# A new order of TensorE's units and new list priorities in a fused attention and MLP kernel

## The chip, the cores and the metric

The kernel runs on one core of a Trainium2 chip. The metric is device time in microseconds (us), from the start of one execution to its end. Three runs of the kernel before took 804.34, 805.24 and 806.07 us.

## The reference, cut to what matters

```python
# x: 2048 tokens x 512; 32 heads of 128; 8 memory rows; segments of 32 tokens
def _A_ref(x, mem0, Wq, Wk, Wv, Wo, seg_len):
    mask = (idx[:, None] < M) | (idx[:, None] >= idx[None, :])
    mem = mem0
    for s in range(n_seg):                       # 64 segments, one after the other
        xs = x[:, s * seg_len:(s + 1) * seg_len, :]
        h = jnp.concatenate([mem, xs], axis=1)   # 8 + 32 rows
        q, k, v = (einsum('btd,dhe->bhte', h, W) for W in (Wq, Wk, Wv))
        p = _softmax(where(mask, einsum('bhqe,bhke->bhqk', q, k) * scale, -1e9))
        o = einsum('bhte,hed->btd', einsum('bhqk,bhke->bhqe', p, v), Wo)
        mem = o[:, :M, :]                        # goes into the next segment
        outs.append(o[:, M:, :])
h  = x + _A_ref(_layernorm(x), ...)
y  = _layernorm(_layernorm(h))
h2 = h + gelu(y @ w1 + b1) @ w2 + b2             # 512 -> 1792 -> 512
```

Weights, inputs and output are bf16. The eight memory rows make the 64 segments a chain: no segment's queries, keys and values are complete before the output projection of the one before it.

## The kernel before, in words

**Segments.** The kernel treats the last 24 tokens of each memory-plus-segment window apart from the rest. For segment s, the tile `hT` holds, transposed, 24 token rows and the 8 memory rows. The other 8 rows of the segment (`hB`) don't depend on memory and are projected for four segments at once, one group of four ("bank") ahead; this work is called F.

TensorE's work in a segment is cut into *units*, with these names. Q0, Q1, K0, K1, V0, V1 (`passes`, line 796): a projection of half of the heads, four units each; a unit is four matmuls of 512 columns side by side in four column tiles of 32 (written 128\*32 in the profile). F0 and F1: in three segments of a bank, the Q, K or V projection of `hB`, four units each, of the same form; in the fourth segment `wo_B` (line 1112), eight units in F1's name. In the last bank F0 and F1 are the MLP's first matmuls instead (`w1_first`, line 1233), plain 128\*128 matmuls. In the first bank F is four dummy matmul units (`warm`, line 765). SC0 and SC1 (`sc_mm`, line 963): scores of the memory queries, for half of the heads each; behind each stands a softmax (`sc_softmax`: maximum `nmc` L972 on VectorE, exponentials `EC` L976 on ScalarE, reciprocal `rsc` L979, product `PC` L982 and a transpose into `PTC` L983 on VectorE). PV0 and PV1 (`pv_c`, lines 994 and 998): probabilities times values for these; they and PVA run in row tiles of 32 (32\*128). SA (`sa_mm`, line 1025): scores of the 24 token rows, one unit; its softmax ends in `PTA`. PVA (`pv_a`, line 1055), two units: probabilities times values of the segment before. WO (`wo`, line 1083): the output projection, eight units; VectorE transposes its result (`TT`, L1095) and adds its halves into the memory rows of the next `hT` (L1089).

Projections go from PSUM to `kq` (a copy on ScalarE or VectorE, lines 814 and 815) and through a VectorE transpose (L839) into `KALL` and `QT`; queries are copied into `ZC`. V goes to `VS`.

**Order.** TensorE's order is written out: `ORDERS` gives for each *place* a list of `unit.from.to`. A place is a1 to a3 for segments 1 to 3, m0 to m3 for segments 4 to 59 by s modulo 4 (14 segments each), and z60 to z63 for the last four. Segment 0 (`START`) and the MLP behind segment 63 have orders of their own. `TURNED` says in which places a projection goes through its four units backwards; where two neighbouring units use the same weights, the second doesn't load them.

The order of the other engines comes from a list scheduler (`Sched.schedule`) that runs when the kernel is built. It takes operations by rank, that is by the longest modelled way from an operation to the end, plus a *bonus* from the table `BONUS` by the kind of its output and its place ("PTC1@m0"). It places each at the earliest free time of its engine, by modelled durations (`dur`), by a modelled signal time (`HOP`) and a cost for a turn between tile forms (`SWITCH`). Some copies may go to ScalarE or VectorE, whichever ends earlier. On the chip each engine runs its list in order and waits on semaphores.

```python
heapq.heappush(heap, (-o.rank - BONUS.get(o.key, BONUS.get(o.kind, 0.0)), pos[o], o.gidx, o))   # Sched.schedule
...
for n, lo, hi in [(u, int(x), int(y)) for u, x, y in (w.split(".") for w in ORDERS.get(place(s), "").split())]:
    S.take((s, n), lo, hi)          # TensorE's own list
```

`align` counts TensorE's instructions (`ni` of each unit: 8 for a projection unit, 4 if weights are kept, 32 for SC and for a half of PVA, 40 for PV, 16 for WO, 64 for SA). It counts in blocks of 256 (`FETCH_N`), and pads the first units of each m0 segment with repeated weight loads until the third unit's place in its block is `LOCK` = 106.

Of the kernel before, what the change touches and what calls it, by code (L numbers as in the profile page):

```python
# [1599 lines left out]
```

## Time and profile before

| what | value |
|---|---|
| median of three runs (lowest, highest) | 805.24 us (804.34, 806.07) |
| span of the profiled execution | 802.2 us |
| median less span | 3.0 us |
| TensorE busy | 775.9 us, 97% of the span |
| VectorE busy | 600.7 us, 75% |
| ScalarE busy | 558.0 us, 70% |
| GpSimd busy | 90.1 us, 11% |
| mean granted TensorE clock | 0.998 |
| LDWEIGHTS instructions | 20880, 423.1 us |

The span runs from the first to the last instruction of the profiled execution; that execution's time as a run isn't given on its own, so its span is set against the median of the runs. A matmul's end in the profile is modelled, and neighbours overlap: for pace, one reads the starts. In the timeline a row with "x8" merges eight matmuls, two units of four. Lines 547 and 796 are both projection units, with and without a weight load. The segments begin at about 48 us and end at about 700 us; the MLP follows.

### The profile page before, as it was taken

To read this page: it belongs to the slowest core of one execution; us is meant where nothing else is said; L and a number is where in the kernel's file an instruction comes from. 1 tells how busy PE (TensorE), PEld (TensorE's weight loads), DVE (VectorE), ACT (ScalarE), POOL (GpSimd) and SP (SyncE) were. 2 spreads that over 40 slices of the span, in tenths; PEclk is the share of its full clock that TensorE was granted. 3 is DMA by queue.
4 is the path that set the end of the run, shared out by engine and by line. 5 is a ranking of instruction groups with operands and counts; after the bars stand their busy time and mean duration, and the time that the engine had idled before them with its cause. 6 is when DMAs were issued, how large, how long until landed. Compare 5 with 4: busy or idle time off the path is not lost.

```text
span 802.2 us, 46835 instructions
## 1 busy us (share of the span) xinstructions
PE 775.9 (97%) x21699; PEld 423.1 (53%) x20880; DVE 600.7 (75%) x1847; ACT 558.0 (70%) x1580; POOL 90.1 (11%) x211
## 2 busy tenths in 40 slices
PE   2899999999999999999999999999999999999998
PEld 1455555555555555555555555555555555644444
DVE  3277878888888888888888888888888888732311
ACT  1557777777777777777778777777777777773342
POOL 5022000010001010101010101000000000020700
PEclk9999999999999999999999999999999999999999
DMA  9961010201111121102010202010212112074300
GB/s 367 394 174 24 4 37 11 45 12 37 26 33 30 30 33 27 36 19 42 19 43 15 49 12 50 13 37 20 50 25 56 51 38 59 17 232 127 86 27 26
DMA packets 65555, 48.77 MB, mean 61 GB/s; under 512 B 28996, under 2 KB 63308, under 8 KB 63820
## 3 DMA queue, kind: packets, MB, share of 16 engines
q1 hardware_dynamic: 65024, 45.50, 20.3%
q8 instruction: 166, 2.72, 1.4%
q14 instruction: 33, 0.27, 0.1%
q10 hardware_dynamic: 332, 0.27, 0.1%
HBM read 31.08 MB, written 8.13 MB: 49 GB/s over the span
## 4 chain that ended last, share of the span: by engine, by line
PE 91%; DMA 3%; DVE 2%; ACT 1%; SPq 1%; issue 1%; POOL 0%; DVEq 0%; ACTq 0%
PE ps L796 43%; PE ps L1083 15%; PE ps L547 8%; PE quad L1465 6%; PE ps L1451 5%; DMA WQ<-in_A_Wq_dram 3%; PE ps L1112 3%; PE quad L994 3%; PE quad L1055 2%; PE ps L1025 2%; PE ps L1233 1%; PE ps L963 1%; PE quad L963 1%; SPq L708 1%; PE quad L998 1%
## 5 line engine op out<-in xcount | busy, mean ns | idle before, releaser
L1083 PE MATMUL ps<-WO,OT 128*32 128x256 bf16 x4224 | 140.6, 274 | 0.1
L796 PE MATMUL ps<-WQ,hT 128*32 128x512 bf16 x1864 | 131.6, 379 | 0.7 <-DVE hT L1089 0.5
L796 PE MATMUL ps<-WV,hT 128*32 128x512 bf16 x1364 | 125.2, 381 | 0.0
L796 PE MATMUL ps<-WK,hT 128*32 128x512 bf16 x1700 | 123.6, 380 | 0.1
L815 ACT ACTIVATE kq<-ps 128x512 bf16<-128x512 f32 x160 | 95.4, 597 | 32.3 <-PE ps L796 26.4
L1083 PEld LDWEIGHTS ps<-WO,OT 128*32 128x32 bf16 x4224 | 100.9, 96 | 26.5 <-ACT OT L814 5.5
L814 ACT CAST kq<-ps 128x512 bf16<-128x512 f32 x162 | 94.8, 585 | 19.9 <-PE ps L796 13.1
L814 ACT CAST OT<-quad 128x128 bf16<-128x128 f32 x191 | 84.4, 442 | 27.0 <-PE quad L998 18.8
L839 DVE STREAM_TRANSPOSE KALL<-kq 128x256 f32<-128x256 f32 x160 | 71.2, 445 | 15.0 <-ACT kq L814 11.8
L796 PEld LDWEIGHTS ps<-WQ,hT 128*32 128x32 bf16 x1864 | 50.3, 97 | 58.8 <-issue 19.0
L861 POOL COPY ZC<-QTB 128x256 bf16<-128x256 bf16 x64 | 25.6, 401 | 477.2 <-PE ps L963 455.7
L796 PEld LDWEIGHTS ps<-WK,hT 128*32 128x32 bf16 x1700 | 45.8, 96 | 56.9 <-issue 14.5
L547 PE MATMUL ps<-WV,hT 128*32 128x512 bf16 x684 | 67.6, 379 | 0.0
L796 PEld LDWEIGHTS ps<-WV,hT 128*32 128x32 bf16 x1364 | 38.4, 97 | 47.3 <-issue 36.6
L839 DVE STREAM_TRANSPOSE QT<-kq 128x256 f32<-128x256 f32 x128 | 57.0, 445 | 6.5 <-ACT kq L815 1.9
L1454 ACT ACTIVATE WQ<-ps,b1t 128x512 bf16<-128x512 f32 x42 | 28.9, 688 | 46.6 <-PE ps L1451 46.6
L1095 DVE STREAM_TRANSPOSE TT<-ps 128x256 f32<-128x256 f32 x66 | 29.7, 450 | 36.3 <-PE ps L1083 36.1
L814 ACT CAST VS<-ps 128x512 bf16<-128x512 f32 x65 | 38.1, 586 | 26.6 <-PE ps L796 26.5
L814 DVE CAST VS<-ps 128x512 bf16<-128x512 f32 x63 | 41.8, 663 | 5.4 <-PE ps L796 5.4
L1541 DVE TENSOR_TENSOR WV<-quad,WV 128x512 bf16<-128x512 f32 (+1 forms) x16 | 10.5, 672 | 45.6 <-PE quad L1465 45.6
L982 DVE TENSOR_TENSOR PC<-EC,rsc 128x128 bf16<-128x128 f32 x128 | 39.7, 310 | 4.3
L1112 PE MATMUL ps<-WO,OTB 128*32 128x512 bf16 x512 | 42.1, 381 | 0.4 <-issue 0.2
(163 smaller groups left out, 1432.1 us busy)
## 6 DMA issues: line engine op xcount, KB each, us to landing
WV<-in_A_Wv_dram SPq DMA_DIRECT2D x4, 1024.0 KB, 8.5
WK<-in_A_Wk_dram SPq DMA_DIRECT2D x4, 1024.0 KB, 14.2
WQ<-in_A_Wq_dram SPq DMA_DIRECT2D x4, 1024.0 KB, 24.7
WO<-in_A_Wo_dram SPq DMA_DIRECT2D x8, 512.0 KB, 9.4
v_last<-VSB SPq DMA_DIRECT2D x60, 64.0 KB, 2.9
...
```

The source lines that it names most:

```text
L547: return e.add_instruction(mybir.InstMatmult(name="I-%d" % (4000000 + _kept[0]), engine=mybir.EngineType.PE, start_tensor_calc=start, stop ...
L796: ins = e.matmul(o, l, m, start=(k == 0), stop=(k == DC - 1), tile_position=(0, 32 * j), skip_group_check=True)
L814: return {"act": (lambda e: e.copy(out, src), t_act(n, ps_)), "dve": (lambda e: e.tensor_copy(out, src), 0.16 + 1.042e-3 * n * fast)}
L815: return {"act": (lambda e: e.mul(out, src, scale_), t_act(n, ps_)), "dve": (lambda e: e.tensor_scalar(out, src, scale_, None, ALU.mult), ...
L839: S.op("dve", lambda e: e.transpose(out, src), reads=[("kq", i)], writes=[key], dur=t_dve(256) + 0.02, after=after)
L982: S.op("dve", lambda e: e.tensor_tensor(PC[:, r].rearrange("p t a -> p a t"), EC[:, r], bc, ALU.mult), reads=[("EC", r), ("rsc", r)], writ ...
L1083: ins = e.matmul(ps[bank][32 * j:32 * j + 32, 0:256], lhs(slot(h)), wo_cols(h, b), start=(k == 0), stop=(k == 15), tile_position=(0, 32 * ...
L1095: S.op("dve", lambda e: e.transpose(tt.rearrange("p c q t -> p (c q t)"), ps[bank][:, 0:256]), reads=[("ps", bank)], writes=[("TT", par)], ...
L1112: ins = e.matmul(ps[bank][32 * j:32 * j + 32, :], OTB[:, bk % 2, slot(h), :], WO[:, h, :], start=(k == 0), stop=(k == 7), tile_position=(0 ...
L1451: ins = e.matmul(ps[bank][:, 0:SBT], W1[:, cc, fc * P:(fc + 1) * P], hnT_of(k)[:, cc, :], start=(cc == 0), stop=(cc == DC - 1))
L1454: S.op("act", lambda e: e.activation(gT[:, fc, :], ps[bank][:, 0:SBT], ACTF.Gelu_apprx_tanh, bias=b1t[:, fc:fc + 1], scale=1.0), reads=[(" ...
L1465: S.op("pe", lambda e: e.matmul(quad[:, t, :], lhs, W2[:, fc, :], **flags), reads=[("W2", part_of(fc))] + gT_keys(k, fc), writes=[("ps", t ...
```

## The change

The diff replaces three tables and a handful of modelled durations. Nothing is added to or taken from the computation, except that one addition on GpSimd becomes a multiplication and an addition in the same instruction (the two layer norms in a row taken exactly).

- `ORDERS` and `TURNED`: a new list for every place. The four places that make up most of the run are shown in full, before and after.
- `BONUS`: nearly all entries are new (three are shown); before, most lay within 15 of zero and some at 40 either way, after, most lie near 40, 0 or -40.
- `SWITCH` and five durations of TensorE units get smaller, one gets larger. The planner alone reads them.

```diff
-SWITCH = 0.1
+SWITCH = 0.095
...
-BONUS = {"": 3.88, "EC0": 19.37, "EC0@a1": -40, ...
+BONUS = {"": -40, "EC0": -49.35, "EC0@a1": -8.2, ...
...
-TURNED = {..., "m0": "F0 F1 Q0 V0", "m1": "K0 K1 Q1 V0", "m2": "F0 K0 K1 V0", "m3": "F1 K0 K1 Q1 V0", ...}
+TURNED = {..., "m0": "F0 F1 Q0 V0", "m1": "K0 Q0 Q1 V0 V1", "m2": "K0 K1 Q0 V0", "m3": "K0 K1 Q1 V0", ...}
 ORDERS = {...
-  "m0": "Q0.0.2 Q1.0.1 Q0.2.4 K0.0.4 Q1.1.4 K1.0.4 SC0.0.1 V0.0.1 V1.0.2 V0.1.2 V1.2.3 V0.2.4 SC1.0.1 V1.3.4 F0.0.1 PVA.0.2 PV0.0.1 F0.1.4 WO.0.2 PV1.0.1 WO.2.8 F1.0.4 SA.0.1",
-  "m1": "K0.0.1 Q0.0.2 K0.1.2 Q0.2.4 K0.2.3 Q1.0.1 K0.3.4 Q1.1.4 K1.0.4 SC0.0.1 V1.0.1 V0.0.2 V1.1.2 V0.2.3 V1.2.3 V0.3.4 SC1.0.1 V1.3.4 F0.0.1 PVA.0.2 PV0.0.1 F0.1.4 WO.0.2 PV1.0.1 WO.2.8 F1.0.3 SA.0.1 F1.3.4",
-  "m2": "K0.0.2 Q0.0.4 K0.2.4 Q1.0.4 K1.0.4 SC0.0.1 V1.0.1 V0.0.2 V1.1.2 V0.2.3 V1.2.3 V0.3.4 SC1.0.1 V1.3.4 F0.0.2 PVA.0.2 PV0.0.1 F0.2.4 WO.0.2 PV1.0.1 WO.2.8 SA.0.1 F1.0.4",
-  "m3": "K0.0.1 Q0.0.2 K0.1.2 Q0.2.4 K0.2.4 Q1.0.4 K1.0.4 SC0.0.1 V1.0.1 V0.0.1 V1.1.2 V0.1.3 V1.2.3 V0.3.4 SC1.0.1 F1.0.1 V1.3.4 PVA.0.2 PV0.0.1 F1.1.5 WO.0.1 PV1.0.1 WO.1.8 F1.5.7 SA.0.1 F1.7.8",
+  "m0": "Q1.0.1 Q0.0.4 K0.0.4 Q1.1.4 K1.0.4 SC0.0.1 V1.0.1 V0.0.2 V1.1.3 V0.2.4 V1.3.4 SC1.0.1 F0.0.2 PVA.0.2 PV0.0.1 F0.2.4 WO.0.2 PV1.0.1 WO.2.8 SA.0.1 F1.0.4",
+  "m1": "K0.0.1 Q0.0.2 K0.1.2 Q0.2.4 K0.2.4 Q1.0.1 K1.0.1 Q1.1.4 K1.1.4 V1.0.1 SC0.0.1 V0.0.3 V1.1.2 V0.3.4 SC1.0.1 V1.2.3 PVA.0.2 V1.3.4 F0.0.2 PV0.0.1 F0.2.4 WO.0.1 PV1.0.1 WO.1.8 F1.0.2 SA.0.1 F1.2.4",
+  "m2": "Q0.0.1 K0.0.1 Q0.1.4 K0.1.4 Q1.0.4 K1.0.4 SC0.0.1 V0.0.1 V1.0.1 V0.1.2 V1.1.2 V0.2.4 SC1.0.1 F0.0.1 V1.2.3 F0.1.2 V1.3.4 PVA.0.2 PV0.0.1 F0.2.4 WO.0.2 PV1.0.1 WO.2.8 SA.0.1 F1.0.4",
+  "m3": "K0.0.1 Q0.0.2 K0.1.2 Q0.2.4 K0.2.4 Q1.0.3 K1.0.1 Q1.3.4 K1.1.3 SC0.0.1 K1.3.4 V1.0.1 V0.0.2 V1.1.2 V0.2.3 V1.2.3 V0.3.4 SC1.0.1 F1.0.2 V1.3.4 PVA.0.2 PV0.0.1 F1.2.4 WO.0.1 PV1.0.1 WO.1.8 F1.4.6 SA.0.1 F1.6.8",
...
-  "z60": "... K1.0.4 SC0.0.1 V1.0.1 V0.0.4 V1.1.2 SC1.0.1 V1.2.4 PVA.0.2 PV0.0.1 F0.0.4 WO.0.2 PV1.0.1 WO.2.8 SA.0.1 F1.0.4",
-  "z61": "... SC1.0.1 V1.3.4 PVA.0.2 PV0.0.1 F0.0.4 WO.0.2 PV1.0.1 WO.2.8 F1.0.4 SA.0.1",
-  "z62": "... SC1.0.1 V1.3.4 PVA.0.2 PV0.0.1 F0.0.4 WO.0.2 PV1.0.1 WO.2.8 SA.0.1 F1.0.4",
+  "z60": "... V1.0.1 V0.0.2 SC0.0.1 F0.0.1 V0.2.3 SC1.0.1 V1.1.2 V0.3.4 V1.2.4 PVA.0.1 F0.1.3 PVA.1.2 PV0.0.1 F0.3.4 PV1.0.1 WO.0.8 SA.0.1 F1.0.4",
+  "z61": "... SC1.0.1 PVA.0.1 V1.3.4 F0.0.2 PVA.1.2 PV0.0.1 F0.2.4 WO.0.1 PV1.0.1 WO.1.8 F1.0.4 SA.0.1",
+  "z62": "... SC1.0.1 V1.3.4 F0.0.1 PVA.0.2 F0.1.2 PV0.0.1 F0.2.4 WO.0.1 PV1.0.1 WO.1.8 SA.0.1 F1.0.4",
...
 def passes(...):      # a projection unit
-                         dur=0.215 * len(parts), ...
+                         dur=0.2165 * len(parts), ...
 def sc_mm(...):       # SC:      dur 0.13 -> 0.12
 def pv_c(...):        # PV0, PV1: dur 0.16 -> 0.145
 def sa_mm(...):       # SA:      dur 0.25 -> 0.235
 def pv_a(...):        # PVA half: dur 0.13 -> 0.108
 def nat(bk):
-            S.op("pool", lambda e: e.tensor_scalar(rs, ag[:, 1:2], 1e-5, None, ALU.add), ...
+            S.op("pool", lambda e: e.tensor_scalar(rs, ag[:, 1:2], 1.00001, 1e-10, ALU.mult, ALU.add), ...
```

More of the change, by code (lines that the diff above doesn't have):

```diff
@@ L36 @@
 HALVES = ("kq", "KA", "QT", "ZCm", "VS", "nmc", "EC", "rsc", "PC", "PTC", "OTm", "KB", "QTB", "VSB")
-BONUS = {"": 3.88, "EC0": 19.37, "EC0@a1": -40, "EC0@a2": 0, "EC0@a3": 2.13, "EC0@m0": 4.48, "EC0@m1": 40, "EC0@m2": 0, "EC0@m3": -7.71,
[48 rows of a table removed]
-         "kq4@m1": 0, "kq5": 4.41, "kq5@m0": -40, "kq5@m1": 17.96, "maskA": 40, "maskAF": 28.24, "maskCF": 40, "maskR": 4.63, "nma": -6.56,
[22 rows of a table removed]
+BONUS = {"": -40, "EC0": -49.35, "EC0@a1": -8.2, "EC0@a2": -39.39, "EC0@a3": -1.75, "EC0@m0": -40, "EC0@m1": -1.1, "EC0@m2": 0.75, "EC0@m3": -61.4,
[70 rows of a table added]
 LEAN = 0.36
@@ L117 @@
          ("SA", 0, 99))
-TURNED = {"a1": "K0 Q1 V0", "a2": "K0 Q0", "a3": "V1", "m0": "F0 F1 Q0 V0", "m1": "K0 K1 Q1 V0", "m2": "F0 K0 K1 V0", "m3": "F1 K0 K1 Q1 V0", "z60": "F1 K0 K1 V0 V1", "z61": "Q0 Q1 V0", "z62": "F1 K0 Q0", "z63": "K0 K1 V0 V1"}
-ORDERS = {"a1": "Q0.0.3 K1.0.1 Q0.3.4 K0.0.2 Q1.0.1 K0.2.4 Q1.1.4 K1.1.4 SC0.0.2 V0.0.3 V1.0.1 V0.3.4 V1.1.2 SC1.0.1 V1.2.4 PVA.0.2 PV0.0.1 F1.0.1 WO.0.2 PV1.0.1 WO.2.8 F1.1.2 SA.0.1 F1.2.4",
[10 rows of a table removed]
+TURNED = {"a1": "Q0 V0 V1", "a2": "K1 V0 V1", "a3": "K1 Q0 Q1 V0 V1", "m0": "F0 F1 Q0 V0", "m1": "K0 Q0 Q1 V0 V1", "m2": "K0 K1 Q0 V0", "m3": "K0 K1 Q1 V0", "z60": "K0 V0", "z61": "K1 Q0 Q1 V0", "z62": "K0", "z63": "K0 K1 Q0 Q1 V0"}
+ORDERS = {"a1": "SC0.0.1 Q0.0.1 K1.0.1 K0.0.2 Q0.1.4 K0.2.4 Q1.0.4 K1.1.4 V1.0.1 SC0.1.2 V0.0.2 V1.1.2 V0.2.4 SC1.0.1 PVA.0.1 V1.2.4 PVA.1.2 PV0.0.1 WO.0.1 PV1.0.1 WO.1.8 F1.0.3 SA.0.1 F1.3.4",
[10 rows of a table added]
 BANK = dict(K0=7, K1=4, Q0=6, Q1=5, V0=5, V1=6, F0=4, F1=5, FB=5, SC0=0, SC1=7, SA=4, WO=6)
@@ L800, in passes @@
                 u = S.op("pe", f, reads=[(key, r, cc) for _, key, r, _, _ in parts] + reads, writes=[("ps", p[3]) for p in parts],
-                         dur=0.215 * len(parts), mode=MC, ni=4 + 4 * len(parts))
+                         dur=0.2165 * len(parts), mode=MC, ni=4 + 4 * len(parts))
                 u.pad, u.held = pad, (slot, cc)
@@ L966, in sc_mm @@
             S.op("pe", f, reads=[("ZCm", par, r), ("ZCb", par), ("KA", par, r)] + [("KB", k, q_) for k in range(2) for q_ in range(2)],
-                 writes=[bkey], dur=0.13, mode=MC, ni=32)
+                 writes=[bkey], dur=0.12, mode=MC, ni=32)
         def sc_softmax(s, r, bank):
@@ L1000, in f @@
                 return ins
-            S.op("pe", f, reads=[("VS", s % 3, r), ("PTC", r)] + [("VBD", bk % 2, j) for j in range(4)], writes=QK, dur=0.16, mode=MR, ni=40)
+            S.op("pe", f, reads=[("VS", s % 3, r), ("PTC", r)] + [("VBD", bk % 2, j) for j in range(4)], writes=QK, dur=0.145, mode=MR, ni=40)
             src = quad[:, :, 64 * r:64 * r + 64].rearrange("p j (i q) -> p j i q", i=4)
@@ L1027, in f @@
                 return ins
-            S.op("pe", f, reads=[("QT", 0), ("QT", 1), ("KA", par, 0), ("KA", par, 1)], writes=[("ps", bank)], dur=0.25, mode=MC, ni=64)
+            S.op("pe", f, reads=[("QT", 0), ("QT", 1), ("KA", par, 0), ("KA", par, 1)], writes=[("ps", bank)], dur=0.235, mode=MC, ni=64)
             v = o.rearrange("p (a t) -> p a t", a=8)
@@ L1057, in f @@
                     return ins
-                S.op("pe", f, reads=[("VS", par, half), ("PTA", s % 2)], writes=QK, dur=0.13, mode=MR, ni=32)
+                S.op("pe", f, reads=[("VS", par, half), ("PTA", s % 2)], writes=QK, dur=0.108, mode=MR, ni=32)
         def pv_a_ev(s):
@@ L1135, in nat @@
             S.op("dve", lambda e: e.bn_aggr(ag, st2[:, i, :]), reads=[("st2", i)], writes=[("ag2", bk)], dur=0.15)
-            S.op("pool", lambda e: e.tensor_scalar(rs, ag[:, 1:2], 1e-5, None, ALU.add), reads=[("ag2", bk)], writes=[("rs2", bk)], dur=0.2)
+            S.op("pool", lambda e: e.tensor_scalar(rs, ag[:, 1:2], 1.00001, 1e-10, ALU.mult, ALU.add), reads=[("ag2", bk)], writes=[("rs2", bk)], dur=0.2)
             S.op("pool", lambda e: e.tensor_tensor(rs, rs, cneg[:, 0:1], ALU.pow), reads=[("rs2", bk), "cneg"], writes=[("rs2", bk)], dur=0.58)
```

152 rows, old and new, of tables (BONUS, ORDERS) are left out of this document.

## The prediction

> **What bounds the kernel now.** I read the page first (busy shares, then the chain that ended last), then the timeline of TensorE through one group of four segments, then VectorE's timeline beside it.
>
> ```profile
> span 802.2 us, 46835 instructions
> ...
> PE 775.9 (97%) x21699; PEld 423.1 (53%) x20880; DVE 600.7 (75%) x1847; ACT 558.0 (70%) x1580; POOL 90.1 (11%) x211
> ...
> PE 91%; DMA 3%; DVE 2%; ACT 1%; SPq 1%; issue 1%; POOL 0%; DVEq 0%; ACTq 0%
> ```
>
> TensorE is busy for 97% of the span and makes 91% of the chain; the rest of the chain is mostly the weights' load at the start. The change takes no matmul away and adds none, so it can only move the time in which TensorE waits or turns from one tile shape to another. Busy time doesn't show that (a matmul of 512 columns is drawn 0.39 us long, but its neighbour starts 0.22 us later); the starts do. Here is the second half of an m2 segment (34):
>
> ```profile
> 395.64 0.30 PE L963 MATMUL ps<-KALL,ZC 128*32 128x64 bf16 x16
> 395.77 0.39 PE L796 MATMUL ps<-WV,hT 128*32 128x512 bf16 x4
> 395.98 0.61 PE L796 MATMUL ps<-WV,hB 128*32 128x512 bf16 x8
> 396.52 0.37 PE L1055 MATMUL quad<-PTA,VS 32*128 32x32 bf16 x32
> 396.74 0.30 PE L994 MATMUL quad<-PTC,VS 32*128 32x16 bf16 x16
> ...
> 397.02 0.61 PE L796 MATMUL ps<-WV,hB 128*32 128x512 bf16 x8
> 397.49 0.62 PE L1083 MATMUL ps<-WO,OT 128*32 128x256 bf16 x16
> 398.04 0.26 PE L994 MATMUL quad<-PTC,VS 32*128 32x16 bf16 x16
> ```
>
> Read start to start: SC1 takes 0.13, one quarter of a projection (four matmuls of 512) 0.21 to 0.22, PVA 0.22, PV0 with its second part 0.28. The two F units at 395.98 take 0.54 where two quarters take 0.43: the turn from column tiles (128*32) to row tiles (32*128) costs 0.11. Two WO units at 397.49 take 0.55, again 0.44 and a turn. From SC1 to PV1 this is 2.40 us, and every piece is TensorE's own pace. So the steady state is close to full, and what an order can win is small.
>
> It can lose, though, where a distance on TensorE falls below what the other engines need. The first such distance is the same one in m0 (segment 32):
>
> ```profile
> 375.12 0.30 PE L963 MATMUL ps<-KALL,ZC 128*32 128x64 bf16 x16
> ...
> 377.52 0.26 PE L994 MATMUL quad<-PTC,VS 32*128 32x16 bf16 x16
> ```
>
> 2.40 us as well. What the softmax between SC1 and PV1 needs is read from VectorE in segment 34 and from segment 2, where the load of PV1's weights waited for it:
>
> ```profile
> 396.03 0.29 DVE L972 TENSOR_REDUCE nmc<-ps 128x2 f32<-128x128 f32 x1
> ...
> 397.09 0.17 DVE L979 RECIPROCAL rsc<-smc 128x2 f32<-128x2 f32 x1
> 397.29 0.31 DVE L982 TENSOR_TENSOR PC<-EC,rsc 128x128 bf16<-128x128 f32 x1
> 397.63 0.25 DVE L983 STREAM_TRANSPOSE PTC<-PC 128x64 f32<-128x64 f32 x1
> ```
> ```profile
> 64.66 0.30 PE L963 MATMUL ps<-KALL,ZC 128*32 128x64 bf16 x16
> ```
> ```profile
> 66.62 0.25 DVE L983 STREAM_TRANSPOSE PTC<-PC 128x64 f32<-128x64 f32 x1
> ```
> ```profile
> 66.92 0.17 PEld L994 LDWEIGHTS quad<-PTC,VS 32*128 32x128 bf16 x16 [0.24 <-DVE PTC L983]
> ```
>
> The transpose ends at 397.88, 2.24 after SC1's start, and the weights follow 0.05 later (66.87 to 66.92): 2.29 us. The operations stand back to back with ScalarE's exponentials between 396.32 and 397.09, so no priority shortens this. The old orders leave 0.11 us of room.
>
> The second distance is the border between segments: WO ends, VectorE turns and adds its result (TT, hT), and the next segment's first projection starts. What lies behind WO covers it.
>
> ```profile
> 410.04 1.13 PE L1112 MATMUL ps<-WO,OTB 128*32 128x512 bf16 x8
> 410.78 0.59 PE L1025 MATMUL ps<-KALL,QT 128*32 128x32 bf16 x32
> 411.20 0.41 PE L1112 MATMUL ps<-WO,OTB 128*32 128x512 bf16 x4
> 411.43 0.84 PE L796 MATMUL ps<-WQ,hT 128*32 128x512 bf16 x12
> ```
> ```profile
> 657.70 0.78 PE L1112 MATMUL ps<-WO,OTB 128*32 128x512 bf16 x8
> ...
> 658.85 0.40 PE L796 MATMUL ps<-WQ,hT 128*32 128x512 bf16 x4
> ```
> ```profile
> 379.10 1.04 PE L796 MATMUL ps<-WK,hB 128*32 128x512 bf16 x16
> 379.96 0.42 PE L1025 MATMUL ps<-KALL,QT 128*32 128x32 bf16 x32
> 380.32 0.40 PE L796 MATMUL ps<-WK,hT 128*32 128x512 bf16 x4
> ```
>
> Behind m3's WO stand three wo_B units and SA. The border takes 1.15 us (657.70 to 658.85) or more, 1.39 at 410.04, where two units of 0.22 last 0.74: TensorE stood 0.3 us ahead of SA. Its own work there is 3 x 0.22 + 0.25 = 0.90, so 0.25 to 0.49 is lost in each m3. The m0 to m1 border takes 1.22 with SA last.
>
> **The change part by part.** The four places m0 to m3 run 14 times each; a bank below is one of each.
>
> *SC1 to PV1 in m0.* The old list has V1's last quarter, four F units and two WO units there, the new one four F units and two WO units: V1's last quarter is now ahead of SC1. 2.40 less 0.22 is 2.18, under the 2.29 needed: TensorE waits 0.11 for PTC1. Bounds: 0, were the chain as short as 2.18; 0.3, were a copy queued ahead of it. In segment 2 the whole distance was 2.26 (64.66 to 66.92), so I take 0.10, between the two readings of 0.08 and 0.11. *In m3* five units and one WO unit stand where six and one stood: 0.13 + 3 x 0.22 + 0.11 + 0.22 + 0.28 + 2 x 0.22 + 0.33 = 2.17. Again 0.10. Behind the waiting PV1 are six or seven WO units, then TT and the next segment's projections, so each wait shifts everything.
>
> *m1.* The new list puts V1's last quarter and two F units between PVA and PV0. TensorE then turns to row tiles three times instead of twice: one more 0.11 into them, and one more way out of them, which the rows show only together with PV0 (0.28). Bounds 0.11 and 0.20; I take 0.15. In return SC0 to PV0 gets longer; nothing is late there in m2 (PVA to PV0 0.22), so this buys little.
>
> *Border m3 to m0.* The new list has two wo_B units, SA, two wo_B units: 0.86 + 0.25 = 1.11 us of cover for 1.15. That would win the 0.25. But the stand ahead of SA isn't a wait for VectorE: at 410.04 it falls inside a unit, after part of its matmuls. The code counts TensorE's instructions in blocks of 256 and pads to hold their place; by that count the old block ends inside the seventh wo_B unit, where the gap is. By the same count of the new lists (8 a projection unit, 4 where weights are kept; 32 a score, PVA half; 40 PV; 16 WO; 64 SA) the block begins in PVA's second half as before, and 10 + 40 + 16 + 16 + 40 + 112 + 16 = 250 instructions later comes SA: it ends at SA's start, after 0.28 + 0.44 + 0.33 + 0.10 + 0.24 + 1.54 + 0.43 = 3.4 us against the old 3.5. So the gap stays, some 0.2 on average, and takes back what the cover wins. I take 0; bounds -0.28 (border 1.15 with four units) and +0.15. The Trainium skill, "Runtime: NRT & Kernel Launch", section "Instruction fetch mechanics", states that crossing a block of 256 instructions is mostly hidden; by that rule the 0.28 would be won. The trace's 0.74 us for two units doesn't agree, at least where a block is used up in 3.5 us.
>
> *Border m0 to m1.* SA moves ahead of F1, as in m2: 1.22 becomes 1.15, -0.07.
>
> *K1 to SC1.* In m1 and m2 one projection quarter less stands between them.
>
> ```profile
> 394.01 0.29 PE L963 MATMUL quad<-KALL,ZC 128*32 128x64 bf16 x16
> ```
> ```profile
> 394.86 0.45 DVE L839 STREAM_TRANSPOSE KALL<-kq 128x256 f32<-128x256 f32 x1
> ```
>
> K1 ended where SC0 began; KALL is there at 395.31, and 0.05 later the score may start: 1.35 after K1. The new distance is six quarters and one score, 1.41. I take 0, upper bound 0.23 in each (the 0.29 of nmc queued ahead of the transpose), lower bound 0.
>
> Per bank: 0.10 + 0.10 + 0.15 + 0 - 0.07 = 0.28; times 14: **+3.9 us**.
>
> *z60 to z62.* Their F units are plain 128*128 matmuls, and turning to these costs too:
>
> ```profile
> 677.19 1.51 PE L1083 MATMUL ps<-WO,OT 128*32 128x256 bf16 x48
> 678.63 1.04 PE L1233 MATMUL ps<-hnT,kq 128*128 128x512 bf16 x4
> 679.59 0.38 PE L1025 MATMUL ps<-KALL,QT 128*32 128x32 bf16 x32
> ```
>
> Six WO units take 1.44 instead of 1.32, four F units 0.96 instead of 0.86: 0.2 for a stretch of its own. The new lists cut these units into more stretches: z60 puts one between SC0 and V0 and one between PVA's halves (0.2 each), but has PV1 right behind F0, which saves a turn of 0.11; z61 and z62 put one more around PVA, 0.2 and a turn of 0.11. That is 0.3 each: **+0.9 us** (bounds 0.3 and 1.4).
>
> *The rest.* a1 to a3 run once and wait on chains already: -0.8 to +0.5, I take **-0.3**. The lists of the start and of the tail stay as they are; behind TensorE's chain there (the start's weight loads, the tail's 128*128 matmuls) priorities move only work beside it: 0, with bounds of 0.5 either way, the size of one late kq copy. The new second operand of one addition (rs2), 16 times on POOL, 11% busy, is read only by the norms of the tail, and POOL has 89% of its time free: 0. The changed durations are the planner's numbers and cost nothing themselves.
>
> Sum: 802.2 + 3.9 + 0.9 - 0.3 = 806.7 us of span. The median of the runs shown, 805.24, is 3.0 above the span; carried over: **809.7**, rounded to 809.5.
>
> **The rivals.** *A, the fetch gap closes.* If the block at m3's end is there in time, the border becomes 1.15 with one more unit in it: 0.28 x 14 = 3.9 less, 805.6, no change. This is what the section of the skill named above would give. For it: at 657.70 the border was at 1.15 already. Against: the new block is used up 0.1 us sooner. It decides when the gap ahead of SA falls under 0.04.
>
> *B, faster.* A, and PV1 waits for nothing because the score's chain gets under 2.18: another 0.2 x 14 = 2.8 less, 802.8. For it: segment 2's 2.26 is nearer than the 2.29. Against: four operations back to back.
>
> *C, K1 to SC1 binds.* New priorities put nmc of SC0 ahead of KALL's transpose in VectorE's queue, in m1 and m2: 2 x 0.23 x 14 = 6.4 more, 815.9. For it: the margin is 0.06. Against: the planner can order them.
>
> **How the numbers follow.** Forecast 0.50 (809.5; its own range 807 to 812), A 0.20, B 0.16, C 0.14. About 0.2%, 1.6 us, is what a measurement of this kernel can tell from no change. Faster: B and a little of A, 0.20. Same: most of A and the forecast's edge, 0.18. Slower: 0.62. The range leaves out C's end and half of B: 803 to 814.
>
> **What would show it.** In m0 and m3 PV1 starts 2.27 to 2.30 after SC1, its weights waiting for PTC; in m1 three turns to row tiles; the m3 border at 1.3 to 1.5 with a gap at SA's start; the m0 border at 1.15. The forecast is wrong if PV1 comes at 2.18, if the m3 border stays at 1.15, or if a new wait appears at SC1.

## The result, and the profile after

The changed kernel takes 813.47 us (median of four runs, 812.65 to 814.26), the kernel before 805.65 (four runs, 804.34 to 806.22), so it is 7.8 us longer by the medians. The ratio is 1.0089, 95% interval 1.0069 to 1.0109: slower by 0.9%. Three single runs of kernels below, two of opa_late and one of fix2, took 1.1 to 2.5 ms, and neither medians nor ratios take in these slow runs. The profiled executions span 810.9 and 802.2 us, at a mean granted clock of 0.998 both.

From the page of after, busy time by engine and the shares of the chain that ended last:

```profile
span 810.9 us, 46810 instructions
...
PE 781.0 (96%) x21699; PEld 410.0 (51%) x20856; DVE 586.4 (72%) x1791; ACT 582.1 (72%) x1636; POOL 87.3 (11%) x211
...
PE 90%; DMA 3%; DVE 3%; ACT 2%; SPq 1%; issue 1%; DVEq 0%; POOL 0%
```

The number of matmuls is the same, VectorE has 14 us less to do and ScalarE 24 us more (56 copies changed sides), and no other engine has become the bound. The time has to be looked for in the starts of TensorE's units. Cut at the last WO matmul of a segment, the two traces give:

| stretch | before, us | after, us | difference |
|---|---|---|---|
| start and segment 0 | 47.65 | 48.29 | +0.64 |
| segments 1 to 3 | 31.00 | 30.83 | -0.17 |
| segments 4 to 59 | 578.94 | 584.77 | +5.83 |
| segments 60 to 63 | 42.17 | 44.38 | +2.21 |
| tail | 102.45 | 102.66 | +0.21 |

The rows add up to 8.7 us, the difference of the two profiled executions. The period of a place (from WO's end to WO's end, median of 14) went from 10.23, 10.29, 10.23, 10.42 us in m0 to m3 to 10.32, 10.62, 10.28, 10.50: 0.55 per bank, or 7.7 us. That the 56 segments differ by 5.83 only comes from single stands (stretches in which TensorE starts nothing) of 0.2 to 0.9 us, of which the profiled execution of before had 2.5 us more than its medians and that of after 0.7. They are taken up below. That the 7.7 of the periods comes so near to the 7.8 of the runs is chance: the start and the last four segments add 2.85, and the fewer stands take 1.8 away.

**m0 to m1 border.** TensorE's timeline of after at the end of segment 32, then VectorE's:

```profile
382.20 0.42 PE L1024 MATMUL ps<-KALL,QT 128*32 128x32 bf16 x32
382.45 1.06 PE L795 MATMUL ps<-WK,hB 128*32 128x512 bf16 x16
383.63 0.40 PE L795 MATMUL ps<-WK,hT 128*32 128x512 bf16 x4
```
```profile
381.73 0.40 DVE L937 COPY ps<-maskAF 128x256 f32<-128x256 f32 x1
382.16 0.53 DVE L1088 TENSOR_TENSOR opT<-TT 64x96 bf16<-64x96 f32 x2
382.70 0.45 DVE L1094 STREAM_TRANSPOSE TT<-ps 128x256 f32<-128x256 f32 x1
383.19 0.39 DVE L1088 TENSOR_TENSOR hT<-TT 64x32 bf16<-64x32 f32 x2
```

Four units at 382.45 last 0.86 by their own pace, to 383.31, but the next projection starts at 383.63. The border is 1.42 us (median), not 1.15. TT, which could have started at about 382.43, stands behind the addition of the output rows of the segment before (opT, 0.53 us), a result nobody waits for. The planner has the addition end at the moment at which TT can start; on the chip it ends 0.27 us later.

**m3, PV0.** VectorE's timeline of segment 35, and the weight loads with what ended the idle time ahead of them (OT is ScalarE's copy of PV0's result, which WO reads):

```profile
409.53 0.17 DVE L978 RECIPROCAL rsc<-smc 128x2 f32<-128x2 f32 x1 [0.16 <-ACT EC L975]
409.78 0.29 DVE L971 TENSOR_REDUCE nmc<-ps 128x2 f32<-128x128 f32 x1
409.99 0.38 DVE L981 TENSOR_TENSOR PC<-EC,rsc 128x128 bf16<-128x128 f32 x1
410.40 0.24 DVE L982 STREAM_TRANSPOSE PTC<-PC 128x64 f32<-128x64 f32 x1
```
```profile
410.70 0.17 PEld L993 LDWEIGHTS quad<-PTC,VS 32*128 32x128 bf16 x16 [0.16 <-DVE PTC L982]
...
411.50 0.12 PEld L1082 LDWEIGHTS ps<-WO,OT 128*32 128x32 bf16 x8 [0.44 <-ACT OT L813]
```

The maximum for SC1 (409.78) goes ahead of the product for SC0, PTC0 is late, PV0 waits 0.21 for it, and the first WO unit waits 0.10 for OT. From SC1 to PV1 it is 2.44 us (median), where TensorE's own work is 2.17.

**m3 to m0 border**, in TensorE's timeline:

```profile
413.62 0.60 PE L1111 MATMUL ps<-WO,OTB 128*32 128x512 bf16 x8
414.05 0.40 PE L1024 MATMUL ps<-KALL,QT 128*32 128x32 bf16 x32
414.27 0.63 PE L1111 MATMUL ps<-WO,OTB 128*32 128x512 bf16 x8
414.77 1.26 PE L795 MATMUL ps<-WQ,hT 128*32 128x512 bf16 x20
```

Two wo_B units start at 413.62, ahead of SA; from there to the first projection (414.77) it is 1.15 us, now with four units in it. The stand that the prediction placed ahead of SA is there in 2 of 14 banks only (0.41 and 0.54 us; a third shows 0.15).

**m1** shows the third turn, PVA (388.95) and PV0 (390.02) apart:

```profile
388.51 0.29 PE L962 MATMUL ps<-KALL,ZC 128*32 128x64 bf16 x16
388.63 0.39 PE L795 MATMUL ps<-WV,hT 128*32 128x512 bf16 x4
388.95 0.37 PE L1054 MATMUL quad<-PTA,VS 32*128 32x32 bf16 x32
389.25 0.40 PE L795 MATMUL ps<-WV,hT 128*32 128x512 bf16 x4
389.48 0.60 PE L795 MATMUL ps<-WQ,hB 128*32 128x512 bf16 x8
390.02 0.26 PE L993 MATMUL quad<-PTC,VS 32*128 32x16 bf16 x16
...
391.05 0.27 PE L993 MATMUL quad<-PTC,VS 32*128 32x16 bf16 x16
```

SC1 to PV1 is 2.54 us with seven projection and WO units, as many as took 2.40 before.

**z60**, TensorE's weight-and-matmul row with its idle time:

```profile
673.07 0.50 PE L1082 MATMUL ps<-WO,OT 128*32 128x256 bf16 x9
674.12 1.60 PE L1082 MATMUL ps<-WO,OT 128*32 128x256 bf16 x52 [0.54 <-issue]
```

Behind the first WO unit (eight matmuls) and one matmul of the second TensorE stands 0.72 us and waits for nothing that the profile shows ("issue").

### The profile page after: what moved, and what is told of

It is laid out like the page before. It is cut to its first block, busy times and chain, and to the rows that moved or that the text cites. A ratio compares the mean times of both kernels' runs of the same rounds, so it can differ in the third digit from the quotient of the medians.

```text
span 810.9 us, 46810 instructions
## 1 busy us (share of the span) xinstructions
PE 781.0 (96%) x21699; PEld 410.0 (51%) x20856; DVE 586.4 (72%) x1791; ACT 582.1 (72%) x1636; POOL 87.3 (11%) x211
## 3 DMA queue, kind: packets, MB, share of 16 engines
q8 instruction: 166, 2.72, 1.4%
## 4 chain that ended last, share of the span: by engine, by line
PE 90%; DMA 3%; DVE 3%; ACT 2%; SPq 1%; issue 1%; DVEq 0%; POOL 0%
PE ps L795 41%; PE ps L1082 16%; PE ps L546 8%; PE quad L1464 6%; PE ps L1450 5%; DMA WQ<-in_A_Wq_dram 3%; PE ps L1111 3%; PE quad L993 3%; PE ps L1024 2%; PE quad L1054 2%; PE ps L1232 2%; PE ps L962 1%; PE quad L962 1%; DVE TT L1094 1%; SPq L707 1%; PE quad L997 1%
## 5 line engine op out<-in xcount | busy, mean ns | idle before, releaser
L795 PE MATMUL ps<-WK,hT 128*32 128x512 bf16 x1856 | 138.4, 380 | 1.4
L795 PE MATMUL ps<-WQ,hT 128*32 128x512 bf16 x1736 | 124.8, 380 | 0.2
L795 PE MATMUL ps<-WV,hT 128*32 128x512 bf16 x1344 | 117.9, 379 | 0.0
L813 ACT CAST OT<-quad 128x128 bf16<-128x128 f32 (+1 forms) x192 | 85.7, 446 | 30.1 <-PE quad L997 28.0
L814 ACT ACTIVATE kq<-ps 128x512 bf16<-128x512 f32 x144 | 85.9, 597 | 24.8 <-PE ps L795 23.7
L795 PEld LDWEIGHTS ps<-WK,hT 128*32 128x32 bf16 x1856 | 50.4, 97 | 64.3 <-DVE hT L1088 14.1
L795 PEld LDWEIGHTS ps<-WQ,hT 128*32 128x32 bf16 x1736 | 46.2, 97 | 63.4 <-issue 23.3
L813 ACT CAST VS<-ps 128x512 bf16<-128x512 f32 x113 | 65.9, 585 | 7.6 <-PE ps L795 4.8
L546 PE MATMUL ps<-WV,hT 128*32 128x512 bf16 x704 | 66.8, 379 | 0.0
L1450 PE MATMUL ps<-WQ,WK 128*128 128x512 bf16 x168 | 41.7, 380 | 0.0
L795 PE MATMUL ps<-WQ,hB 128*32 128x512 bf16 x512 | 39.6, 389 | 2.1 <-DMA WQ<-in_A_Wq_dram 2.1
```

Of the source, the lines that this page charges most:

```text
L546: return e.add_instruction(mybir.InstMatmult(name="I-%d" % (4000000 + _kept[0]), engine=mybir.EngineType.PE, start_tensor_calc=start, stop ...
L795: ins = e.matmul(o, l, m, start=(k == 0), stop=(k == DC - 1), tile_position=(0, 32 * j), skip_group_check=True)
L813: return {"act": (lambda e: e.copy(out, src), t_act(n, ps_)), "dve": (lambda e: e.tensor_copy(out, src), 0.16 + 1.042e-3 * n * fast)}
L814: return {"act": (lambda e: e.mul(out, src, scale_), t_act(n, ps_)), "dve": (lambda e: e.tensor_scalar(out, src, scale_, None, ALU.mult), ...
L1450: ins = e.matmul(ps[bank][:, 0:SBT], W1[:, cc, fc * P:(fc + 1) * P], hnT_of(k)[:, cc, :], start=(cc == 0), stop=(cc == DC - 1))
```

## The experiments

In all but two of them (lock74 and after74, which change one constant), the planner's lists are made first and then held fast; only what the diff names is moved, on TensorE's list or on one other engine's, and nothing is planned anew. So an edit can't reshuffle the rest. In these kernels the line numbers stand 59 to 63 higher. Ratios are to the kernel before, from runs on the same chip. "Period" is the median of 14 from the trace.

### VectorE's order at the m0 border (m0_opa, opa_late)

```diff
 VectorE's list, m0 (m0_opa):
-  ... pfa  opT(of the m3 segment)  TT  hT  nma  SA ...
+  ... pfa  TT  hT  nma  opT(of the m3 segment)  SA ...
 opa_late: opT stands behind PTC1 of the m1 segment
```

> The changed kernel with one operation of VectorE moved, in the 14 m0 segments: the addition of the output rows of the segment before (opT) stands behind the maximum of SA instead of ahead of TT; every other list as in the changed kernel. Theory (VectorE's order holds the m0 border): TT starts at once when WO has ended, 0.27 us earlier (382.43 instead of 382.70 in segment 32), the border WO to first projection falls from 1.42 to 1.15 us, and the run gets 0.27 x 14 = 3.8 us shorter, 809.7 against 813.5, ratio to the kernel before 1.004. Rival (the border is the weights' or the instructions' fetch, or the moved addition delays the next KALL transpose by as much): border 1.15 but SC0 later by as much, or border still 1.4: no change, ratio 1.009.

> The changed kernel with the addition of m3's output rows moved further back on VectorE than in the run m0_opa: behind PTC1 of the m1 segment, where VectorE has 0.2 to 0.3 us free at a time, instead of behind the maximum of SA. Theory (m0_opa won 0.27 us at the m0 border and gave 0.14 of it back because the 0.53 us addition stood ahead of K1's transpose in m1): border 1.15 and SC0 to SC1 in m1 back at 1.20, so 0.27 per bank shorter than the changed kernel, 3.8 us, ratio to the kernel before 1.004. Rival (m1 is held by something else, a chain through ScalarE): SC0 to SC1 stays at 1.34 or PV1 waits as much, ratio 1.007 as in m0_opa.

Measured: m0_opa 812.61 us, ratio 1.0069 (1.0049 to 1.0089); opa_late 809.69, 1.0042 (1.0027 to 1.0056). In both the m0 border is 1.15 us. In m0_opa the period of m1 fell by 0.12 only (10.62 to 10.50), in opa_late by 0.27 (to 10.35). VectorE in m0_opa, segment 32 to 33:

```profile
382.60 0.42 DVE L1093 TENSOR_REDUCE nma<-ps 128x8 f32<-128x256 f32 x1
383.06 0.52 DVE L1147 TENSOR_TENSOR opT<-TT 64x96 bf16<-64x96 f32 x2
383.59 0.42 DVE L1094 TENSOR_TENSOR SA<-ps,nma 128x256 f32<-128x256 f32 x1
```

and what waited, in ScalarE's timeline and then in TensorE's of the same run:

```profile
384.05 0.42 ACT L1095 ACTIVATE SA<-SA 128x256 f32<-128x256 f32 x1 [0.65 <-DVE SA L1094]
...
385.90 0.59 ACT L873 ACTIVATE kq<-ps 128x512 bf16<-128x512 f32 x1
```
```profile
386.31 0.30 PE L1021 MATMUL quad<-KALL,ZC 128*32 128x64 bf16 x16
386.55 0.83 PE L854 MATMUL ps<-WV,hT 128*32 128x512 bf16 x12
```

The addition, moved, holds up the subtraction for SA's softmax, and ScalarE waits 0.65 us for that ahead of its row of copies. The copy into kq that ends at 386.49 then comes late. Behind SC0 stands V0, whose result goes into the PSUM bank that this copy empties (the kernel gives Q1 and V0 the same one): V0 starts 0.24 us after SC0 instead of 0.12 (medians), and SC1 stands 1.34 us after SC0 instead of 1.20. The chain went through ScalarE, not through K1's transpose as the expectation of opa_late had it. Far back in m1, in opa_late, the addition holds up nobody. Here is VectorE at the same border in opa_late, with TT waiting for WO and for nothing else:

```profile
380.37 0.45 DVE L1153 STREAM_TRANSPOSE TT<-ps 128x256 f32<-128x256 f32 x1 [0.29 <-PE ps L1141]
380.86 0.39 DVE L1147 TENSOR_TENSOR hT<-TT 64x32 bf16<-64x32 f32 x2
```

So one operation's place on VectorE is worth 0.27 us per bank, 3.8 us, about half of what the change lost. The difference of the ratios, 0.0047, is 3.8 us.

### The third turn in m1 (m1_pva), and both repairs together (fix2)

```diff
 m1:
-  SC1.0.1 V1.2.3 PVA.0.2 V1.3.4 F0.0.2 PV0.0.1 F0.2.4 WO.0.1 PV1.0.1
+  SC1.0.1 V1.2.4 F0.0.2 PVA.0.2 PV0.0.1 F0.2.4 WO.0.1 PV1.0.1
 fix2: this, and opT behind the copy of F0 in the m1 segment
```

> The changed kernel with TensorE's m1 list alone changed: V1's last two quarters and two F units ahead of PVA, PVA and PV0 together again, so two turns to row tiles instead of three; the lists of the other engines as in the changed kernel. Theory of the prediction (a third turn costs 0.15 us): SC1 to PV1 2.54 becomes 2.39, above the 2.29 needed, no wait; 0.15 x 14 = 2.1 us shorter, ratio to the kernel before 1.006. Rival (the turn was hidden in a wait for PTC1 or OTm0 that is due anyway): SC1 to PV1 stays at 2.5 or WO waits for OTm0 instead, less than 0.5 us shorter, ratio 1.008 to 1.009.

> The changed kernel with two repairs at once: the addition of m3's output rows late (behind the copy of F0 in the m1 segment), and TensorE's m1 list with PVA and PV0 together. Theory (the losses are separate and add): 0.27 + 0.09 per bank, 5.0 us shorter than the changed kernel, ratio to the kernel before 1.003; what is left is the stand of PV1 in m0 and of PV0 and WO in m3, some 0.19 per bank, and z60. Rival (the places are coupled through VectorE, and what one gives the next waits for): less than half of it, ratio 1.006 or above.

Measured: m1_pva 814.54 us, 1.0086 (1.0065 to 1.0107), not told apart from the changed kernel by time. By the trace m1's period fell by 0.09 (10.62 to 10.53) and SC1 to PV1 from 2.54 to 2.44: PV0 comes 0.20 earlier (SC1 to PV0 1.51, now 1.31), and 0.11 of that comes back as a wait of the first WO unit for OT (PV0 to WO 0.69, now 0.80):

```profile
390.90 0.12 PEld L1141 LDWEIGHTS ps<-WO,OT 128*32 128x32 bf16 x8 [0.40 <-ACT OT L872]
```

The border behind it lengthened from 1.15 to 1.28 in the mean, by single stands at the end of an instruction block.

fix2: 810.41 us, 1.0051 (1.0031 to 1.0071), between the two expectations. m1's period is 10.26, the full 0.36 below the changed kernel, but m2's rises from 10.28 to 10.40, because the border behind m1 grows from 1.15 to 1.25 (median). VectorE there, segment 33:

```profile
391.87 0.39 DVE L1188 TENSOR_TENSOR xr<-xr,oN 128x512 bf16<-128x512 bf16 x1
392.17 0.44 DVE L1153 STREAM_TRANSPOSE TT<-ps 128x256 f32<-128x256 f32 x1
```

The addition opT, now in m1, pushes another addition (xr, the residual's sum) past WO's end, and in 13 of 14 banks TT starts 0.42 us after WO's last matmul instead of 0.32: the loss of the m0 border again, at the next border. In 6 of 14 banks stands in F1 ahead of SA come on top (0.31 to 0.43 us between two matmuls, at a block's end). The gains in m1 do add, and the two repairs together still come out no better than the one, because VectorE and the blocks take the gain back.

### PV1's wait in m0 (m0_v1)

```diff
 m0:
-  ... V0.2.4 V1.3.4 SC1.0.1 F0.0.2 PVA.0.2 ...
+  ... V0.2.4 SC1.0.1 V1.3.4 F0.0.2 PVA.0.2 ...
```

> The changed kernel with TensorE's m0 list alone changed: V1's last quarter behind SC1 as in the kernel before; the lists of the other engines as in the changed kernel. Theory of the prediction (PV1 waits 0.10 for PTC1 when only 2.18 us of work lie between): SC1 starts 0.22 earlier, SC1 to PV1 goes from 2.28 to 2.40 with no wait, the period of m0 falls by 0.10; 1.4 us shorter in all, ratio to the kernel before 1.007. Rival (2.28 is TensorE's own pace with the new lists, or K1 to SC1 takes the wait): period of m0 unchanged, ratio 1.009.

Measured: 813.13 us, 1.0076 (1.0054 to 1.0098). SC1 to PV1 went from 2.28 to 2.50, not 2.40, and m0's own period didn't fall (10.32 to 10.39). The weight loads of the first two WO units and of PV1, then VectorE and ScalarE:

```profile
379.56 0.37 PEld L1141 LDWEIGHTS ps<-WO,OT 128*32 128x32 bf16 x16 [0.41 <-DVE rsc L1037]
380.13 0.17 PEld L1052 LDWEIGHTS quad<-PTC,VS 32*128 32x128 bf16 x16 [0.21 <-DVE PTC L1041]
```
```profile
379.65 0.24 DVE L1041 STREAM_TRANSPOSE PTC<-PC 128x64 f32<-128x64 f32 x1
```
```profile
379.18 0.27 ACT L872 CAST OT<-quad 128x128 bf16<-128x128 f32 x1
```

PTC1 is ready at 379.89, and PV1's weights load 0.24 us later, so PV1 doesn't wait for it; its 0.21 of idle time is there in undisturbed segments too. What waits is the first WO unit: it starts 0.33 us after F0's last unit, where m1 shows 0.23 (medians). It reads OT, whose copy ends at 379.45; rsc, which the profile names, is no input of WO. In the kernel before, m0 had three F units between PV0 and WO to cover this copy, the new list has two. So the 0.10 doesn't come from V1's place alone: the period stays, as the rival had it, if not for the rival's reason. The run also shows the coupling. WO came later against VectorE's list (the output addition oBn, which stood 1.5 us ahead of WO's end, stands 1.7 ahead of it), TT found VectorE free sooner, and the m0 border fell to 1.26 and m1's period by 0.16.

### Three or four units behind m3's WO (m3_five)

```diff
 m3:
-  PV0.0.1 F1.2.4 WO.0.1 PV1.0.1 WO.1.8 F1.4.6 SA.0.1 F1.6.8
+  PV0.0.1 F1.2.5 WO.0.1 PV1.0.1 WO.1.8 F1.5.7 SA.0.1 F1.7.8
```

> The changed kernel with TensorE's m3 list alone changed: three wo_B units instead of two between PV0 and WO, and so three behind WO beside SA instead of four, as in the kernel before; the lists of the other engines as in the changed kernel. Theory now (blocks of instructions cost nothing at the m3 border in most banks; the border is 1.15 us of VectorE's work, and the fourth unit covered 0.22 of it): SC1 to PV1 keeps PV0's wait of 0.21 for PTC0 and loses WO's wait of 0.10 for OTm0, the border waits 0.22 again, the m3 to m0 part of a bank gets 0.12 longer, 1.7 us in all, ratio to the kernel before 1.011. The prediction's step (the end of a block takes back what the fourth unit covers): border alike with three and four units, 0.10 per bank shorter, 1.4 us, ratio 1.007.

Measured: 816.16 us, 1.0108 (1.0085 to 1.0130), which the time alone doesn't tell from the changed kernel's 1.0089. The trace does: m3's period is 10.58 against 10.50, as the new theory had it (0.08 longer where 0.12 was expected: SC1 to PV1 grew by 0.09 for a unit of 0.22, so 0.13 of the waits went, not 0.10). With three units the border is 1.15 as with four, and TensorE stands in it, ahead of the first projection:

```profile
374.59 0.41 PE L1170 MATMUL ps<-WO,OTB 128*32 128x512 bf16 x4
375.09 0.83 PE L854 MATMUL ps<-WQ,hT 128*32 128x512 bf16 x12
```

0.50 us for one unit of 0.22. The border is VectorE's 1.15 us, and the fourth unit covers 0.22 of it.

### Where the instruction blocks end (lock74, cand, cand74, after74)

lock74 is the kernel before with the constant LOCK at 74, so that each block of 256 instructions begins 32 instructions later in the work; after74 is the changed kernel with the same.

```diff
-LOCK = 106
+LOCK = 74
```

> The kernel before with its blocks of 256 TensorE instructions laid 32 instructions further on (LOCK 74 instead of 106), nothing else. By its traces a fetch of a block starts 0.4 to 1.1 us after the block ahead of it is entered and takes 0.9 to 1.4 us, and no block is used up in less than some 3.55 us. Theory (a block can't be used up faster than that; TensorE stands where its work in a block is shorter): the shortest blocks of a bank hold 2.72 and 2.88 us of work here, so 0.83 + 0.67 us are lost in each bank beside some 0.25 that were lost already, about 1.3 x 14 = 18 us longer, ratio about 1.02. Rival (the prediction's A: the crossing of blocks is mostly hidden, and the stand at the m3 border is something else): no change, ratio within 1.000 to 1.003.

Measured: 805.36 us, 0.9983 (0.9970 to 0.9997). Nothing is lost; the four medians are 10.22, 10.29, 10.23, 10.43. Blocks of 2.76 us (m2) and 2.85 (m0), which the theory had lose 0.7 and more each, were used up without a stand. And the m3 border, three units, still takes 1.15. The block now ends inside SA, and TensorE stands behind the last wo_B unit, ahead of the projection (0.50 from one start to the next):

```profile
368.26 0.60 PE L1112 MATMUL ps<-WO,OTB 128*32 128x512 bf16 x8
368.69 0.40 PE L1025 MATMUL ps<-KALL,QT 128*32 128x32 bf16 x32
368.92 0.41 PE L1112 MATMUL ps<-WO,OTB 128*32 128x512 bf16 x4
369.42 1.26 PE L796 MATMUL ps<-WQ,hT 128*32 128x512 bf16 x20
```

The theory of a fixed least time for a block falls. The Trainium skill, "Runtime: NRT & Kernel Launch", section "Instruction fetch mechanics", has the crossing mostly hidden; this run agrees.

cand takes the kernel before and puts four wo_B units behind m3's WO without making PV1 wait, and SA ahead of F1 in m0:

```diff
 m0:
-  WO.2.8 F1.0.4 SA.0.1
+  WO.2.8 SA.0.1 F1.0.4
 m3:
-  PV0.0.1 F1.1.5 WO.0.1 PV1.0.1 WO.1.8 F1.5.7 SA.0.1 F1.7.8
+  PV0.0.1 F1.1.4 WO.0.2 PV1.0.1 WO.2.8 F1.4.6 SA.0.1 F1.6.8
```

> The kernel before with two of the new ideas and none of the new priorities: in m0 SA ahead of F1, and in m3 four wo_B units behind WO instead of three, with PV1 behind the second WO unit instead of the first, so that SC1 to PV1 keeps its 2.39 us; the lists of the other engines as in the kernel before. Theory now (the borders are VectorE's 1.15 us; TensorE's own cover decides): m3's border is covered but for 0.04, 0.21 won, m0's border 1.22 becomes 1.15, 0.07 won; 0.28 x 14 = 3.9 us shorter, ratio to the kernel before 0.995. Rival one (the end of an instruction block takes the border's gain): only the 0.07, ratio 0.999. Rival two (the softmax chains on VectorE are the next bound, as in the changed kernel: the gained time comes back as waits of PV0 and PV1): ratio 1.000 or above.

Measured: 806.90 us, 1.0015 (0.9991 to 1.0039). The softmax took nothing back: SC1 to PV1 is 2.40 in m3, whose period falls to 10.22. But TensorE stands in SA of nearly every m3, by 0.63 us in the median. Segment 23:

```profile
287.19 0.60 PE L1171 MATMUL ps<-WO,OTB 128*32 128x512 bf16 x8
287.62 0.18 PE L1084 MATMUL ps<-KALL,QT 128*32 128x32 bf16 x2
289.03 0.37 PE L1084 MATMUL ps<-KALL,QT 128*32 128x32 bf16 x30 [1.23 <-issue]
```

Two of SA's 32 matmuls are the last of a block, the next 30 come 1.4 us later, and their weight loads too, for no reason on any other engine. So here the Trainium skill's rule does not hold: at this place a crossing costs 0.63 us. And m0's border stayed at 1.22 with SA ahead of F1: the projection's weights wait for hT there, so SA's place alone didn't win the 0.07.

> The run cand with its blocks of 256 TensorE instructions laid 32 instructions further on (LOCK 74), nothing else. In cand TensorE stood 0.63 us (median) at SA of each m3, where a block ended that begins in PVA's second half and is used up in 3.4 us; in lock74 the block there goes from PV0 to the middle of SA and holds 3.6 us of work, and its instructions came in time. Theory (a block's instructions are there about 3.5 us after the block ahead of it is entered: the fetch starts 1.05 after, takes 1.0 and is used 1.45 after its end): the block holds 3.41 us in cand74, TensorE stands 0.1 to 0.2 instead of 0.63, and 0.1 of the 0.2 us that the fourth wo_B unit covers is kept: ratio to the kernel before 0.995 to 0.999, m3 and m0 together 20.5 to 20.6 us against 20.65. Rival (the stand at SA isn't the block's end but follows SA, wherever the block ends): as cand, m3 and m0 together 21.0 us, ratio 1.0015 or above.

> The changed kernel with its blocks laid 32 instructions further on (LOCK 74), nothing else. The blocks from PV0 to SA then hold 3.26 us of work in m1 and 3.35 in m3; in the kernel before, at the same place, 3.60 and 3.6. Theory (3.5 us are needed): TensorE stands some 0.25 us at SA in each m1 and 0.15 in each m3 beside what it loses already, 0.4 x 14 = 5.6 us longer, ratio to the kernel before 1.014 to 1.017; z60 falls from 11.7 to about 10.9 us, if its stand of 0.7 between the second and third WO unit is the end of a block too. Rival (the crossing of blocks is mostly hidden, and single stands come by chance): no change, ratio 1.009.

Measured: cand74 811.17 us, 1.0050 (1.0028 to 1.0072), and the stand went with the block's end into the middle of SA (behind 14 to 18 of its 32 matmuls, in all banks but one), 0.73 us in the median instead of 0.1 to 0.2. That it is the block's end is shown; its size was missed. after74: 816.16, 1.0122 (1.0100 to 1.0143), 2.7 us longer than the changed kernel where 5.6 were expected: m3's SA stands 0.35, m1's not at all, though its block is the shorter (3.28 us). z60 stayed at 11.78 us, with stands at the new block's end and in SA.

### Do data transfers delay the fetch? (cand_vbd, before_vbd)

```diff
+        for o in self.rec:
+            if o.is_dma and o.key == "VBD@m2":
+                g = [p for p in pe if p.tag == (o.tag[0] + 1, "WO")][0]
+                o.deps = sorted(o.deps + [g], key=lambda d: d.gidx)
```

> The run cand with one dependency more: the four transfers that fill VBD (64 KB each, issued by SyncE in each m3) wait for the first WO unit of that segment, so that their packets come about 2 us later; nothing else. In cand they run from 2.2 us ahead of WO's end to its end, and the fetch of TensorE's block that is needed at SA starts 1.8 us (median) after the block ahead of it is entered, where other blocks have 0.6 to 1.1; in the two m3 segments with the fewest packets of data in that time (142 and 215, against 277 to 528) it starts after 0.8 and 1.1 and SA doesn't stand. Theory (the fetch waits behind the packets of VBD): the fetch starts 1.0 after, the stand at SA falls from 0.63 to 0.1 or less, m3 and m0 together from 21.0 to 20.5 us, 0.5 x 14 = 7 us less than cand at most, ratio to the kernel before 0.993 to 0.997. Rival (the transfers only move on and the next block's fetch, in m0, waits instead, or the stand is from the short block alone): m3 and m0 together stay above 20.8, ratio 0.999 to 1.002.

> The kernel before with the same dependency for VBD's transfers and nothing else. Theory (single stands at the m3 border come from fetches behind VBD's packets): the stands of 0.2 to 0.3 us that 3 of its 14 m3 borders show at a block's end go away, 0.7 us in all; the stand in PVA of one m3 stays, since it falls in the time of the transfers into v_last; ratio 0.998 to 1.000. Rival (moved transfers hit other fetches): 1.000 to 1.003.

Measured: cand_vbd 806.82 us, 1.0007 (0.9990 to 1.0025); before_vbd 806.59, 1.0009 (0.9990 to 1.0028). The packets of VBD came about 2 us later, from 2.5 us after the block ahead of SA's is entered, and in 12 of 14 banks no data moved between that entry and the start of the fetch. It still started 1.6 us or more after the entry in 7 of 14, and SA stood there; 0.28 us is the median of all, against 0.63 in cand. Segment 23, one of them:

```profile
287.06 0.18 PE L1088 MATMUL ps<-KALL,QT 128*32 128x32 bf16 x2
287.68 0.37 PE L1088 MATMUL ps<-KALL,QT 128*32 128x32 bf16 x30 [0.44 <-issue]
```

m3 and m0 together take 20.69, between the two expectations, and m2 got 0.1 longer than in cand (10.42 to 10.32) by stands at m1's border. before_vbd went rather as its rival had it: the m3 border's mean fell from 1.21 to 1.16, and the m1 border's rose from 1.22 to 1.29. The packets aren't the cause, or not alone. What makes a fetch start late stays open.

No kernel here beats the one before by much. lock74 is 0.2% faster at the edge of what can be told; cand and cand_vbd can't be told from it.

## Why the prediction was right or wrong, step by step

The direction held, and so did the wide range; the sum did not. The forecast stood 4.5 us above the kernel before, measured are 7.8, and 813.47 lies outside the forecast's own range of 807 to 812. That it lies inside 803 to 814 is luck, by 0.5 us: the range was widened upwards for rival C, whose mechanism didn't occur. One sign that was to show the forecast wrong came: the m3 border stayed at 1.15. And the steps' errors partly offset each other. Per bank, by the medians of the starts:

| step | predicted, us | measured, us |
|---|---|---|
| m0, SC1 to PV1 (predicted: PV1 waits for PTC1) | +0.10 | +0.10 |
| m3, SC1 to PV1 (predicted: PV1 waits for PTC1) | +0.10 | +0.27 |
| m1, third turn | +0.15 | +0.15 |
| border m3 to m0 | 0 | -0.22 |
| border m0 to m1 | -0.07 | +0.20 |
| m2 | 0 | +0.05 |
| sum | +0.28 | +0.55 |

**SC1 to PV1 in m0: right in size, not in the wait.** It is 2.28 us, 0.10 more than TensorE's own work. Here is TensorE in segment 32 of after:

```profile
379.53 0.61 PE L795 MATMUL ps<-WK,hB 128*32 128x512 bf16 x8
380.07 0.62 PE L1082 MATMUL ps<-WO,OT 128*32 128x256 bf16 x16
380.62 0.26 PE L993 MATMUL quad<-PTC,VS 32*128 32x16 bf16 x16
```

Two F units take 0.54, where in m1 two take 0.45 (390.26 to 390.71): the first WO unit is 0.09 late, for OT, as in m0_v1. Two WO units and a turn take 0.55, the pace that the prediction read in m2, so PV1 adds no wait. PTC1 is ready 2.21 us after SC1's start. With the 0.05 that the weights need after it, the chain alone would have held PV1 to about 2.26, as the prediction had it: two limits lie at nearly the same place, and that the size came out is partly luck. *In m3 the step failed*: PV1 doesn't wait there either (PTC1 is ready 0.2 ahead of it). PV0 waits 0.21 for PTC0, which the prediction didn't reckon with, and the first WO unit 0.10 for OT. The rows of before gave no warning, with PV0 2.58 us after SC0 and nothing late; the new priorities put the maximum for SC1 in between. m2's 0.05, too, stands ahead of the first WO unit (0.29 instead of 0.24).

**m1's turn: right** in size; 0.09 of the 0.15 can be had back (m1_pva).

**m3 to m0 border: wrong step.** "So the gap stays, some 0.2 on average, and takes back what the cover wins." What the prediction read as a stand at a block's end at 410.04 was in most banks VectorE's 1.15 us (the median of the border before is 1.16, the mean 1.21), and with four units 0.22 was won (m3_five). Rival A's mechanism, the gap closing, held in the changed kernel, but not because crossings are always free: in cand, with four units behind WO and without the new waits, the stand is there, 0.63. The likely reason is that the waits of PV0 and WO stretch the block from PVA to SA to 3.62 us; no run takes these waits alone out of the changed kernel, so this is argued, not shown.

**m0 to m1 border: wrong step.** "SA moves ahead of F1, as in m2: 1.22 becomes 1.15, -0.07." The border of 1.15 can be had, as opa_late shows, but not by SA's place alone (cand: 1.22). The failed assumption is that VectorE is free when WO ends. The prediction weighed the priorities only where two operations of the same softmax met; an addition that no one waits for, placed by the planner with no room to spare, was not looked for. That is the largest miss, 0.27 x 14 = 3.8 us.

**K1 to SC1: right**, no new wait (1.20 us from SC0 to SC1 in m1). Rival C is out. **Rival B** is out too: the chain stayed at 2.21 and 0.08 for the weights, not under 2.18.

**z60 to z62:** 0.9 predicted. z60 takes 10.36 us before and 10.84 in the two executions of these lists without the long stand (m0_v1, m3_five), 11.6 to 12.2 in six others; z61 rose by 0.26 and z62 by 0.40 (0.13 in m0_v1). So the turns are about the 0.9; the stand at the block's end (0.72 here) and z63 (+0.26) were not in the sum. In z63 PV0 starts 0.28 later than PVA's own 0.22 would have it: it waits for ScalarE's copy of V into VS, which ends at 704.53, while PTC0 is ready at 704.31.

**Start:** 0 predicted, +0.64 measured. It is 47.6 to 47.7 in the six profiled executions built on the kernel before and 47.8 to 50.7 in the eight built on the changed one, so it goes with the new lists of the other engines; which operation was not tried. **Segments 1 to 3** (-0.3 predicted, -0.17) and the tail (0, +0.21) were close.
